# Keeping the first batch on chip in a fused FFT filter and MoE kernel: block transposes on VectorE in place of two trips through DRAM

## The chip, the cores and the metric

The kernel runs on one core of one Trainium2 chip. The metric is the device time of one execution in microseconds (us). Every time below is a median of fast runs; the span that a profile shows is about 2 us shorter than the time of the same run. Kernels that are compared ran on the same chip, with the kernel before run beside them.

A core has a matrix engine (TensorE, "PE" in the profile; its weight loads are "PEld"), VectorE ("DVE"), ScalarE ("ACT"), GpSimd ("POOL") and a queue engine (SyncE, "SP"). A "q" behind a name means the engine's instruction queue, which waits and issues DMAs.

## The reference

```python
# x (8, 3008, 256); filt_r, filt_i (1505, 256); w_in (256, 2048); w_out (2048, 256); alpha (2048,)
X = np.fft.rfft(x, axis=1)
y = np.fft.irfft(X * (filt_r + 1j * filt_i)[None], n=3008, axis=1)   # a circular filter along the sequence
h = y.reshape(24064, 256) @ w_in
s = np.sin(alpha * h)
out = (h + s * s / (alpha + 1e-09)) @ w_out
```

The kernel splits the FFT of length 3008 into 47 x 64. Per batch it does a first small transform (matmul `pa`), a second one with twiddles (`pb`), a product with the filter (`p`), and the two inverses (`pc`, `pd`), whose result `y` feeds the dense part. Between the first and the second transform, and again between the two inverses, the data must change its layout: what was a row index becomes a partition. The kernel before writes to DRAM and reads back for that. The dense part is one hidden matmul (`ph`), a cosine on ScalarE, a "snake" on VectorE (`v`), and a projection (`po`). It works in chunks of 512 tokens, and a chunk is 8 steps. To evict, below, is to copy a matmul's result (`ps`) to a tile that later work reads. The spectral work of a later batch is dealt out between the steps of the dense part of an earlier one, so that TensorE always has something to do. Only batch 0 has nothing to hide behind.

## The kernel before

The order in which batch 0 and batch 1 are worked, with cuts:

```python
FUSED = 2                                   # batches from this one on use the "fused" product
class Spectral:
    def first(self, i):                     # pa, then t1 to DRAM
        ...
        if j == 3:
            nc.sync.dma_start(out=self.d1_rows[:, 8 * ch:8 * ch + 8, :], in_=self.t1)
    def load_t2(self, g): ...               # t2 <- d1, the other layout
    def forward(self, u):                   # pb, evicted to xf
        ...
        if self.fused:                      # the other half of the partitions, by DMA
            for p in range(2):
                nc.sync.dma_start(out=self.xs[u][64 * p:64 * p + 64, :, :],
                                  in_=self.xf[u][64 - 64 * p:128 - 64 * p, :, :])
    def product(self, u):                   # one product if fused, two if not
        for k in range(1 if self.fused else 2): ...
    def cross(self, u):                     # fused: xs * f1, then added to p
        ...
    def inverse(self, w):                   # pc: one matmul a slice if fused, two if not; then g to DRAM
        ...
    def load_t4(self, ch): ...              # t4 <- d2
    def last(self, u): ...                  # pd, evicted to y

def load_x(b, ch):                          # on GpSimd's queue
    ...
    if b == 1: after(ins, marks["t4"])      # a wait
    if b > 2:  after(ins, marks["snake"])   # a wait; batch 2 has none
```

An unfused batch multiplies twice and runs 48 inverse matmuls. A fused batch swaps its two halves of 64 partitions by DMA, does three VectorE operations for each block, and runs 24 inverse matmuls. Before the change batches 0 and 1 are unfused.

## Time and profile before

815.3 us, median of 3 runs (814.78 to 815.31). First, two lines of the page of the kernel before: busy time by engine, and the chain of waits that ended last by engine.

```profile
PE 771.4 (95%) x5649; PEld 527.5 (65%) x5649; DVE 652.4 (80%) x1191; ACT 612.8 (75%) x1200; POOL 65.4 (8%) x111
...
PE 88%; DMA 5%; DVE 2%; ACT 2%; issue 1%; POOL 0%; SPq 0%; ACTq 0%; DVEq 0%; POOLq 0%
```

TensorE is the limit. The table of windows of the kernel before shows where it isn't. A row is a stretch in us, its length, then the busy us of each engine (with the number of instructions), TensorE's granted clock as a share of full speed, the mean busy share of the 16 DMA engines, and the rate.

```profile
core 0: us, PE busy (x) PEld busy (x) DVE busy (x) ACT busy (x) POOL busy (x), PEclk, DMA share, GB/s
...
40.00:60.00 20.00, 10.46 (x65) 5.41 (x64) 12.79 (x25) 8.48 (x18) 3.26 (x5) 0.74 0.88 264
60.00:80.00 20.00, 15.70 (x99) 8.91 (x97) 18.51 (x41) 14.71 (x30) 0.00 (x0) 1.00 0.61 145
80.00:100.00 20.00, 20.00 (x153) 13.91 (x151) 15.79 (x27) 15.41 (x31) 7.39 (x12) 1.00 0.71 174
100.00:120.00 20.00, 20.00 (x151) 14.58 (x150) 17.57 (x36) 16.45 (x33) 0.00 (x0) 1.00 0.58 128
```

From 80 us on TensorE is busy all the time; before that it is not. The timeline of TensorE in the kernel before shows the end of the idle start. Columns: start us, duration us, engine, line, operation, out<-in, shape, count; in brackets the idle time before it and what ended it.

```profile
51.38 0.81 PE L230 MATMUL pd<-wi_t,t 96*128 96x94 f16 x8 [8.56 <-DMA t<-d]
...
53.46 1.01 PE L368 MATMUL ph<-y,w 128*128 128x512 f16 x2 [0.17 <-ACT y L136]
```

TensorE stands still for 8.56 us while batch 0 goes through DRAM the second time, and the first hidden matmul (`ph`) starts at 53.46 us. That start is the number to move: everything after about 80 us is a TensorE that never rests, so a start that is earlier by some us should end the run earlier by as much.

### The profile page before, as it was taken

The page shows a single profiled execution, that of the slowest core. Times are in us where ns is not written, and L with a number is a line of the kernel's source. Part 1 is how long each engine was busy: PE and PEld are TensorE (multiplying, and loading weights), DVE is VectorE, ACT ScalarE, POOL GpSimd, SP SyncE. Part 2 cuts the span into 40 slices and gives each one's busy share as a digit, 9 for nine tenths or more (in the row PEclk, how much of TensorE's full clock was granted, in tenths as well). Part 3 has the DMA queues.
Part 4 walks back from the last instruction along what each step waited for, and adds up shares of the span by engine and source line. Part 5 has one row for each costly group of instructions (what it writes and reads, how often), then busy time and mean ns, then how long its engine had stood idle before and what let it go on. Part 6 is the DMA issues. An engine that isn't in the chain of part 4 may idle for free.

```text
span 812.3 us, 16130 instructions
## 1 busy us (share of the span) xinstructions
PE 771.4 (95%) x5649; PEld 527.5 (65%) x5649; DVE 652.4 (80%) x1191; ACT 612.8 (75%) x1200; POOL 65.4 (8%) x111
## 2 busy tenths in 40 slices
PE   5657999999999999999999999999999999999995
PEld 2324676676666776667667676667667676666674
DVE  3669797789978998789987998779987999777772
ACT  4547787788878888778887887778887887777662
POOL 3210300110020000200002000200002000000000
PEclk9779999999999999999999999999999999999998
DMA  9985755466576465644657554654558333411111
GB/s 213 227 260 132 186 113 148 127 137 141 117 185 149 97 144 126 184 95 95 140 159 178 111 104 116 193 127 104 115 139 214 73 91 84 116 37 40 40 40 46
DMA packets 86201, 104.44 MB, mean 129 GB/s; under 512 B 10388, under 2 KB 72868, under 8 KB 86120
## 3 DMA queue, kind: packets, MB, share of 16 engines
q1 hardware_dynamic: 73904, 73.45, 34.3%
q0 software_dynamic: 10288, 29.11, 18.0%
q10 hardware_dynamic: 1928, 0.86, 0.4%
q8 instruction: 44, 0.72, 0.4%
q14 instruction: 37, 0.30, 0.1%
HBM read 58.02 MB, written 49.81 MB: 133 GB/s over the span
## 4 chain that ended last, share of the span: by engine, by line
PE 88%; DMA 5%; DVE 2%; ACT 2%; issue 1%; POOL 0%; SPq 0%; ACTq 0%; DVEq 0%; POOLq 0%
PE po L383 39%; PE ph L368 38%; PE pa L159 4%; PE pc L210 3%; PE pb L179 3%; PE pd L230 2%; DMA t<-d 2%; DMA x<-in_x_dram 2%; DVE v L372 1%; ACT cos L371 1%; DMA d<-t 1%; ACT t L136 1%; DVE p L193 1%; DMA d<-g 0%; DVE t L138 0%
## 5 line engine op out<-in xcount | busy, mean ns | idle before, releaser
L372 DVE SCALAR_TENSOR_TENSOR v<-cos,ph 128x512 f16<-128x512 f32 (+1 forms) x768 | 483.5, 672 | 119.3 <-ACT cos L371 116.2
L371 ACT ACTIVATE cos<-ph 128x512 f32<-128x512 f32 (+1 forms) x768 | 411.5, 591 | 99.7 <-PE ph L368 98.9
L368 PE MATMUL ph<-y,w 128*128 128x512 f16 (+1 forms) x1536 | 388.5, 375 | 0.8 <-DVE y L138 0.6
L383 PE MATMUL po<-w,v 128*128 128x256 f16 x3008 | 389.0, 272 | 0.0
L383 PEld LDWEIGHTS <-v 128*128 128x128 f16 x3008 | 289.2, 98 | 77.7 <-issue 1.7
L368 PEld LDWEIGHTS <-w 128*128 128x128 f16 x1536 | 148.1, 98 | 104.3 <-issue 3.6
L182 ACT CAST xf<-pb 128x512 f16<-128x512 f32 x96 | 56.9, 594 | 20.4 <-PE pb L179 17.3
L389 ACT COPY o<-po 128x512 f32<-128x512 f32 x96 | 55.6, 579 | 17.9 <-PE po L383 16.3
L136 ACT CAST t<-pa 96x512 f16<-96x512 f32 x88 | 51.2, 585 | 22.8 <-PE pa L159 22.6
L159 PE MATMUL pa<-x,wf_t 94*96 94x512 f16 x128 | 51.0, 408 | 11.7 <-DMA x<-in_x_dram 8.3
L230 PEld LDWEIGHTS <-t 96*128 96x128 f16 x512 | 36.1, 99 | 34.3 <-DMA t<-d 11.0
L170 POOL DMA_DIRECT2D t<-d x56 | 37.0, 676 | 251.1 <-PE ph L368 183.6
L230 PE MATMUL pd<-wi_t,t 96*128 96x94 f16 x512 | 43.0, 208 | 11.5 <-DMA t<-d 10.1
L193 DVE TENSOR_TENSOR p<-xf,filt 128x512 f16<-128x512 f16 x120 | 47.8, 418 | 6.3 <-ACT xf L182 6.1
L136 ACT CAST y<-pd 128x376 f16<-128x376 f32 x82 | 39.3, 480 | 17.0 <-PE pd L230 16.6
L136 ACT CAST g<-pc 128x512 f16<-128x512 f32 x65 | 38.4, 590 | 11.8 <-PE pc L210 11.6
L210 PE MATMUL pc<-p,e_t 128*128 128x256 f16 x240 | 44.0, 278 | 2.7 <-DVE p L193 1.5
L179 PE MATMUL pb<-t,d_t 128*128 128x256 f16 x192 | 38.2, 282 | 5.9 <-DMA t<-d 4.9
L118 POOL DMA_DIRECT2D x<-in_x_dram x32 | 17.0, 536 | 262.8 <-PE pc L210 145.9
L138 DVE CAST t<-pa 96x512 f16<-96x512 f32 x40 | 27.2, 680 | 12.6 <-PE pa L159 12.6
L210 PEld LDWEIGHTS <-e_t 128*128 128x128 f16 x240 | 23.0, 99 | 16.2 <-issue 2.5
L200 DVE TENSOR_TENSOR p<-p,xs 128x512 f16<-128x512 f16 x72 | 30.6, 425 | 2.5
(31 smaller groups left out, 155.2 us busy)
## 6 DMA issues: line engine op xcount, KB each, us to landing
d<-t SPq DMA_DIRECT2D x32, 384.0 KB
d<-g SPq DMA_DIRECT2D x64, 192.0 KB
t<-d SPq DMA_DIRECT2D x32, 384.0 KB
x<-in_x_dram POOLq DMA_DIRECT2D x32, 376.0 KB, 6.2
t<-d POOLq DMA_DIRECT2D x56, 192.0 KB, 7.0
xs<-xf SPq DMA_DIRECT2D x144, 64.0 KB
out_dram<-o SPq DMA_DIRECT2D x72, 94.0 KB
w_in<-in_moe_w_in_dram POOLq DMA_DIRECT2D x2, 1024.0 KB, 8.9
```

Of the source, the lines that this page charges most:

```text
L136: marks["act"] = nc.scalar.copy(out=dst, in_=src)
L159: marks["pe"] = nc.tensor.matmul(out=ps[0:NK, :], lhsT=wf_t, rhs=self.x[ch][:, 2 * j:2 * j + 2, :], start=True, stop=True)
L179: nc.tensor.matmul(out=ps[:, i, :], lhsT=d_t[:, s, :], rhs=self.t2[s // 6][:, s % 6, :], start=True, stop=True)
L182: nc.scalar.copy(out=self.xf[u], in_=ps)
L193: marks["prod", u] = nc.vector.tensor_tensor(out=pt, in0=self.xf[u], in1=f_t[k][:, 2 * u:2 * u + 2, :], op=ALU.mult)
L210: nc.tensor.matmul(out=ps[:, i, :], lhsT=e_t[:, k, 2 * w + i, :], rhs=pt[:, i, :], start=(k == 0), stop=(k == len(pr) - 1))
L230: nc.tensor.matmul(out=psv[:, i, :], lhsT=self.t4[ch][:, 4 * half + i, cb * 128:cb * 128 + 128], rhs=wi_t, start=True, stop=True)
L368: nc.tensor.matmul(out=ps[:, 0:n], lhsT=w1[:, cb, jb * 128:jb * 128 + 128], rhs=y_cols[:, cb, c0:c0 + n], start=(cb == 0), stop=(cb == 1))
L371: nc.scalar.activation(out=cs[:, 0:n], in_=ps[:, 0:n], func=AFT.Sin, bias=float(np.pi / 2))
L372: marks["snake"] = nc.vector.scalar_tensor_tensor(out=v[k][:, jb, 0:n], in0=cs[:, 0:n], scalar=-1.0, in1=ps[:, 0:n], op0=ALU.add, op1=ALU. ...
L383: nc.tensor.matmul(out=pso[k][:, t % 2, :], lhsT=v[k][:, jb, 128 * t:128 * t + 128], rhs=w2[:, jb, :], start=(jb == 0), stop=(jb == 15))
L389: nc.scalar.copy(out=o[:, 0:nb, :], in_=pso[k][:, 0:nb, :])
```

## The change

The intent: batch 0 does not leave the chip. Its two changes of layout are done by VectorE as transposes of 32x32 blocks of 32-bit words, each word a pair of fp16 channels. Buffers are shared so that all of it fits; for lack of room the second inverse table of batch 0 lies in a buffer that is needed later, so batch 1 can't use it and becomes fused. Some VectorE work of the start moves to GpSimd: one of the filter copies, the six multiplies that scale `w_in` by alpha, half of the scaling of `w_out`. All engines now run in the order of emission. The core of the diff, with cuts:

```diff
-FUSED = 2
+FUSED = 1
...
+    def turn(dst, src, c0):
+        nc.vector.transpose(out=dst[:, :, c0 % 128:c0 % 128 + 64].bitcast(UINT32).rearrange("p s c -> p c s"),
+                            in_=src.bitcast(UINT32).rearrange("p s c -> p c s"))
...
+    for c0 in (0, 64, 128, 192):
+        turn(t2_0[c0 // 128], t1_0[:, :, c0:c0 + 64], c0)
+    blocks = [(hc, w) for w0 in (0, 3) for hc in range(2) for w in range(w0, w0 + 3)]
...
+    def weights_in(g):
+        js, w32 = w_in32[g]
+        eng = nc.vector if g in () else nc.gpsimd
+        eng.tensor_tensor(out=w1[:, :, js], in0=w32, in1=cos_cols[:, None, js]..., op=ALU.mult)
...
+    for i in range(-1, 12 + 3):                       # batch 0: forward, product, inverse, block by block
+        ... other_half(...)                           # filter copies: i = -1 two on VectorE; i = 5 one on GpSimd, one on VectorE
+        forward_0(i); product_0(i - 1); inverse_0(i - 3)      # in bounds
+        if i == 6:
+            for g in (0,1,2,6,7,8,9,3,4,5):           # w1 multiplies; 6 to 9 are batch 1's x loads
+                ...
+        if i - 3 == 8 + 2:
+            turn_back(0)
+            turn_back(64)
+    turn_back(128)
+    turn_back(192)
...
-                put(13.6 if b == 2 else zp + -44 + 7 * ch, s.load_x, ch)
+                put(2 + 8 + 0.6 if b == 2 else zp + -44 + 7 * ch, s.load_x, ch)
...
-            inv = 22.5 + u if b == 1 else 59 + 2.1 * u if b == 2 else z + -40.8 + 2.3 * u
-            fwd = inv - (1.5 if b == 1 else 6)
+            inv = 17 + 5 + u if b == 1 else 59 + 2.1 * u if b == 2 else z + -40.8 + 2.3 * u
+            fwd = inv - (5 if b == 1 else 6)
...
+                put(fwd + (3 if b == 1 else 4.5), s.cross, u)
```

## The prediction

> **What bounds the kernel now.** TensorE, after a slow start. The window table shows PE busy 97-100% of every stretch from 80 us to 780 us, at full granted clock; before 70 us it is busy about 50 us. Counting columns at 2.4 per ns, the work is about 743 us (estimate from the group list's shapes and counts); about 39 us of it is done by 80 us. So 41 us are lost in the first 80 us, about 17 us in the long middle, 11 us at the end. In the timeline the first hidden matmul (ph) starts at 53.5 us and the first projection at 69.2 us. Before that the chain of waits runs x DMA, first transform (to 17.0), d<-t 4.9 us and t<-d 4.3 us through DRAM, products and inverse (27.0 to 42.8), then d<-g 3.2 us and t<-d 3.8 us: PE stands still 8.6 us before the first pd. Batch 1's x loads cost another 2.1 us at 63.9.
>
> **Removed.** Batch 0's DRAM round trips (about 5.5 and 8.6 us of dead time on the chain, 6.3 MB of DMA traffic while the DMA share is 0.8 to 1.1), the DVE half of the e table; DVE loses the eight w1 multiplies (4.9 us) and half of the w2 scaling (about 2.7 us) to GpSimd; batch 1 loses 24 inverse matmuls (2.6 us of PE), but the second e table by PE adds about as many columns, early, and three ACT evictions (1.02 us).
>
> **Added.** Eight VectorE block transposes of 1024 32-bit elements. The Trainium skill, Vector Engine (DVE) Microarchitecture Reference, section 3.8, says the transpose sustains one element per cycle per lane; no trace here shows it yet. The trace's f32 128x512 multiply takes 0.61 us back to back, so I estimate 1.2 us per transpose, 10 us in all; the last two stand on the chain. GpSimd multiplies: GPSIMD Engine Reference, section 3, has tensor_tensor at about half of VectorE's speed, so about 1.5 to 2 us per w1 group, 10 us, finishing near 40 us, just before the fourth cosine slot, which holds alpha, is needed. Batch 1 gains two VectorE ops per block (24 x 0.42 us, minus 12 products) and 24 swap DMAs.
>
> **Timeline after (estimate).** x landed 11.9; first transform evicted near 16; d_t about 18.5; transposes to 21; then ACT is the limit: 24 evictions of 0.59 plus three tables, 17 us, to 40; two transposes, last, evictions: ph starts at about 44.5, 9 us earlier. Chunk 0 stays VectorE/ACT-bound (15.7 us before, about 15 after). Later stretches are PE-saturated, so the gain stays, with one repayment: batch 1 still does one block per step, where VectorE needs about 2.5 us per step against 2.15 us of PE, so the saved inverse matmuls are not cashed in and 1 to 3 us are lost.
>
> **Predicted: 805.5 us, 8 in 10 between 798 and 811.5; faster by over 2%: 0.14, within 2%: 0.83, slower: 0.03.**
>
> **Shown by:** first ph near 44.5 us; transposes near 1.2 us each; no d<-t, d<-g before it; DMA share lower before 45 us; PE over 95% from about 70 us; VectorE near 100% in batch 1's blocks with PE idle on products or cosines.
>
> **What would make it wrong:** strided 32-bit access making transposes two or more times slower (ph near 49, 809 us); GpSimd slower, holding the cosine slots (later); ACT and VectorE overlapping better, or batch 1 swaps fitting without stall (799 or below).

## More of the kernel before

One more view, the groups of VectorE instructions between 25 and 56 us, for the cost of the filter products and copies before. After the count come the busy us and the mean ns of one.

```profile
L193 DVE TENSOR_TENSOR p<-xf,filt 128x512 f16<-128x512 f16 x24 | 8.7, 420 | 6.3 <-ACT xf L182 6.1
...
L274 DVE COPY filt<-filt 64x1536 f16<-64x1536 f16 x3 | 1.7, 576 | 0.1
```

Back to back they overlap a little: 24 products occupy 8.7 us, 0.36 us each.

## The result, and the profile after

The changed kernel takes 827.79 us (median of 4 runs, 826.39 to 829.48) against 815.3. The ratio is 1.0155, with a 95% interval from 1.0135 to 1.0176: slower by 1.5%, clear of noise, and outside of the predicted range. A ratio here and below is the mean time of one kernel's fast runs over that of the other's of the same rounds, so not quite the ratio of the medians.

The page of the changed kernel, the same two lines:

```profile
PE 778.1 (94%) x5745; PEld 533.0 (65%) x5745; DVE 673.5 (82%) x1187; ACT 617.3 (75%) x1206; POOL 79.1 (10%) x115
...
PE 80%; DVE 7%; DMA 6%; ACT 2%; issue 2%; SPq 1%; POOL 0%; ACTq 0%; DVEq 0%; POOLq 0%
```

VectorE has come onto the chain (2% before, 7% now). To see when the time is lost, compare the two traces at the same place in the program. The dense part is the same 4544 matmuls in the same order in both kernels, so the start of the k-th of them can be set against each other. This table is worked out from the traces; "e15" is the last experiment's kernel, discussed at the end.

| k-th dense matmul | before, us | after, us | difference | e15, us | difference |
|---|---|---|---|---|---|
| 0 (first `ph`) | 53.5 | 55.8 | +2.4 | 47.1 | -6.4 |
| 180 | 94.9 | 96.8 | +1.9 | 87.1 | -7.8 |
| 220 | 101.6 | 111.5 | +9.9 | 93.8 | -7.9 |
| 340 | 125.3 | 136.8 | +11.5 | 119.5 | -5.9 |
| 600 | 169.6 | 180.6 | +10.9 | 164.7 | -4.9 |
| 4543 (last) | 803.7 | 816.7 | +13.0 | 799.7 | -4.1 |

Two things went wrong, and both are early. The dense part starts 2.4 us later instead of 9 us earlier. And 8.0 us are lost between the matmuls 180 and 220, around 100 us. After that the two kernels run alike: the difference grows by another 3.1 us over 700 us.

**The start.** TensorE's timeline of the changed kernel, at the lines that answer to those shown of before:

```profile
51.08 0.81 PE L246 MATMUL pd<-wi_t,t_h 128*128 128x94 f16 x8 [3.53 <-DVE t_h L329]
55.18 0.88 PE L246 MATMUL pd<-wi_t,t_h 128*128 128x94 f16 x8 [3.29 <-DVE t_h L329]
...
55.85 0.63 PE L455 MATMUL ph<-y,w 128*128 128x512 f16 x1
```

The wait for DRAM is gone. A wait for the transposes stands in its place. The groups of VectorE between 17 and 56 us show what VectorE did until then:

```profile
L368 DVE TENSOR_TENSOR p<-xf,filt 128x512 f16<-128x512 f16 x24 | 15.0, 682 | 0.7 <-issue 0.4 <-ACT xf L361 0.2
L329 DVE STREAM_TRANSPOSE t_h<-t_h 128x1024 uint32<-128x1024 uint32 x4 | 8.3, 2180 | 0.0
L329 DVE STREAM_TRANSPOSE t<-t 128x1024 uint32<-128x1024 uint32 x2 | 4.3, 2222 | 0.0
L329 DVE STREAM_TRANSPOSE t_h<-t 128x1024 uint32<-128x1024 uint32 x2 | 3.7, 1925 | 0.4 <-ACT t L148 0.4
L325 DVE TENSOR_SCALAR filt<-filt 64x3072 f16<-64x3072 f16 x2 | 3.5, 1742 | 0.1
```

VectorE is busy without a break and is the limit of the start. A transpose takes 1.9 to 2.2 us, where the prediction had 1.2, and the same 24 products occupy 15.0 us, where they had 8.7 before.

**The stall.** The windows of the changed kernel:

```profile
40.00:60.00 20.00, 12.13 (x115) 8.74 (x114) 16.87 (x24) 10.28 (x21) 3.59 (x5) 0.68 0.04 8
60.00:80.00 20.00, 16.98 (x101) 8.98 (x100) 17.44 (x34) 17.05 (x36) 0.00 (x0) 1.00 0.20 60
80.00:100.00 20.00, 20.00 (x155) 14.10 (x154) 14.79 (x25) 14.25 (x29) 7.40 (x12) 1.00 0.86 192
100.00:120.00 20.00, 13.88 (x93) 9.04 (x92) 13.40 (x29) 12.37 (x25) 0.00 (x0) 0.83 0.34 88
```

From 100 to 120 us TensorE is busy for 13.88 us of 20, where it had been busy all the time. Look at the column of the DMA share too. Before, it was 0.88 in the stretch from 40 to 60 us; now the DMA engines do next to nothing there (0.04), and they are fuller than before from 80 to 100 us (0.86 against 0.71). The traffic was not only taken away, it was pushed together. The timeline and the waits of the changed kernel around 100 us (in the waits: who waited for whom, us in total, times, longest):

```profile
88.61 9.99 SPq L488 DMA_DIRECT2D out_dram<-o  x5
98.70 6.11 SPq L196 DMA_DIRECT2D xs<-xf  x6
...
DVE xs L209 <- DMA xs<-xf: 9.3, 2, 7.9
ACT xf L192 <- DMA xs<-xf: 8.9, 2, 8.4
PE pd L246 <- ACT xf L192: 6.0, 1, 6.0
```

`xs<-xf` is the half swap of batch 1, new with the change. SyncE's queue issues it at 98.70 us, behind output stores, the last of which took 8.58 us to issue; its second half lands at 106.15 us by the chain of waits. Until then ScalarE may not overwrite `xf`, and TensorE waits for ScalarE. In the same time batch 1's `t2` loads land (88 to 94.5 us) and the four loads of batch 2's `x` (96.3 to 102.8 us).

### The profile page after: what moved, and what is told of

Same layout as the page of the kernel before. It is cut to its first block, busy times and chain, and to the rows that moved or that the text cites. A ratio compares the mean times of both kernels' runs of the same rounds, so it can differ in the third digit from the quotient of the medians.

```text
span 825.4 us, 16345 instructions
## 1 busy us (share of the span) xinstructions
PE 778.1 (94%) x5745; PEld 533.0 (65%) x5745; DVE 673.5 (82%) x1187; ACT 617.3 (75%) x1206; POOL 79.1 (10%) x115
## 4 chain that ended last, share of the span: by engine, by line
PE 80%; DVE 7%; DMA 6%; ACT 2%; issue 2%; SPq 1%; POOL 0%; ACTq 0%; DVEq 0%; POOLq 0%
PE po L470 36%; PE ph L455 34%; DMA t_h<-d 3%; PE pd L246 3%; PE pa L169 2%; PE pc L220 2%; DVE v L459 2%; PE pb L189 2%; DMA filt<-in_filt_i_dram 2%; SPq L488 1%; DVE t_h L329 1%; ACT cos_all L458 1%; DMA xs<-xf 1%; DVE p L368 1%; PE pc L378 1%
## 5 line engine op out<-in xcount | busy, mean ns | idle before, releaser
L459 DVE SCALAR_TENSOR_TENSOR v<-cos_all,ph 128x512 f16<-128x512 f32 (+1 forms) x768 | 483.2, 671 | 116.4 <-ACT cos_all L458 113.1
L458 ACT ACTIVATE cos_all<-ph 128x512 f32<-128x512 f32 (+1 forms) x768 | 411.6, 591 | 103.0 <-PE ph L455 102.0
L246 PEld LDWEIGHTS <-t_h 96*128 96x128 f16 (+1 forms) x512 | 35.6, 99 | 39.8 <-issue 7.8
L246 PE MATMUL pd<-wi_t,t_h 96*128 96x94 f16 (+1 forms) x512 | 43.0, 208 | 16.5 <-DVE t_h L329 6.8
L148 ACT CAST t_h<-pa 96x512 f16<-96x512 f32 x75 | 43.9, 587 | 10.2 <-PE pa L169 9.9
L169 PE MATMUL pa<-x,wf_t 94*96 94x512 f16 x112 | 42.3, 381 | 2.7 <-ACT t_h L148 2.5
L209 DVE TENSOR_TENSOR xs<-xs,filt 128x512 f16<-128x512 f16 x84 | 35.0, 417 | 9.3 <-DMA xs<-xf 9.3
L220 PE MATMUL pc<-p,e_t 128*128 128x256 f16 x168 | 32.4, 275 | 3.5 <-DVE p L210 3.4
L203 DVE TENSOR_TENSOR p<-xf,filt 128x512 f16<-128x512 f16 x84 | 35.0, 416 | 0.1
L220 PEld LDWEIGHTS <-e_t 128*128 128x128 f16 x168 | 15.6, 98 | 15.7 <-DVE p L210 4.2
```

What stands on the lines that cost most here:

```text
L148: marks["act"] = nc.scalar.copy(out=dst, in_=src)
L169: marks["pe"] = nc.tensor.matmul(out=ps[0:NK, :], lhsT=wf_t, rhs=self.x[ch][:, 2 * j:2 * j + 2, :], start=True, stop=True)
L220: nc.tensor.matmul(out=ps[:, i, :], lhsT=e_t[:, 2 * w + i, :], rhs=pt[:, i, :], start=(k == 0), stop=(k == len(pr) - 1))
L246: nc.tensor.matmul(out=psv[:, i, :], lhsT=lhsT, rhs=wi_t if self.b else wi0_t, start=True, stop=True)
L458: nc.scalar.activation(out=cs[:, 0:n], in_=ps[:, 0:n], func=AFT.Sin, bias=float(np.pi / 2))
L459: marks["snake"] = nc.vector.scalar_tensor_tensor(out=v[k][:, jb, 0:n], in0=cs[:, 0:n], scalar=-1.0, in1=ps[:, 0:n], op0=ALU.add, op1=ALU. ...
```

## The experiments

The theories for the start: the w1 multiplies on GpSimd slow VectorE (theory C), against products that are slow of themselves (D); and for the transposes strided access (E) against a slow operation (F). For the stall: the swaps wait behind loads on full DMA engines (A), against the fused form as such, its VectorE load or its short distance (B). Times of the kernel before beside each group of runs were 814.8 to 815.2 us. A run where nothing else is said gave the right result.

### e1_x2_late: batch 2's loads put later in the program

```diff
-                put(2 + 8 + 0.6 if b == 2 else zp + -44 + 7 * ch, s.load_x, ch)
+                put(24 if b == 2 else zp + -44 + 7 * ch, s.load_x, ch)
```

> One edit: batch 2's x loads are issued at step 24 instead of 10.6. Theory A (the 6.05 us TensorE stall at 100.5 us comes from batch 1's half swaps, whose DMAs wait behind batch 2's x loads and batch 1's loads on full DMA engines): the stall shrinks to under 2 us and the time falls 5 to 8 us, to about 820. Rival B (the stall is the fused form itself: too few steps between forward and cross, or VectorE load): the stall stays near 6 us and the time stays 826 to 829.

829.77 us, ratio 1.0177 (1.0154 to 1.0199). It decides nothing, because the edit did not do what it was meant to. The trace shows the loads issued at 91.3 to 94.1 us, still right behind the `t2` loads: GpSimd's queue has nothing else to wait for and runs ahead, so the place in the program sets only the order within this queue. To move such a load it must be made to wait for something.

### e2_no_swap: batch 1 without its swap

```diff
-            if self.fused:
+            if b == 1:
+                self.xs[u] = xspool.tile(...)            # no DMA
+            elif self.fused:
...
-        nc.vector.tensor_tensor(out=xs, in0=xs, in1=f_t[1]..., op=ALU.mult)
+        nc.vector.tensor_tensor(out=xs, in0=self.xf[u] if self.b == 1 else xs, in1=f_t[1]..., op=ALU.mult)
```

> Batch 1 leaves its half swap out and multiplies the unswapped tile (wrong result on purpose; VectorE work unchanged, 24 DMAs gone). Theory A: no stall at 100 us, time about 818 to 819. Rival B (VectorE load of the fused form): stall or its equivalent of several us stays between 95 and 135 us, time 825 or more.

Its output is wrong, which doesn't matter for the time. 821.91 us, 1.0078 (1.0055 to 1.0100). The stall is gone: the difference to the kernel before is +4.3 us at matmul 180 and +5.1 at 220. So the swap's DMA is what the stall waits for, and VectorE's load is not, because its work is unchanged. The load has a smaller price: the difference rises to +8.0 us by matmul 280 and falls back to +6.4 by 400, and the time is 3 us above what theory A gave. The short distance between `forward` and `cross` this run doesn't decide; e6 below keeps the distance, and its stop at 100 us is gone.

### e3_w1_on_vector and e4_no_w1_multiply: GpSimd's multiplies

```diff
-        eng = nc.vector if g in () else nc.gpsimd
+        eng = nc.vector
```

> The six w1 multiplies go from GpSimd to VectorE (about 5 us more VectorE work before the first hidden matmul). Theory C (GpSimd's two-input multiplies slow VectorE's two-input products and filter copies in 23 to 37 us): products take 0.36 to 0.45 us each instead of 1.08, the first ph starts about 3 us earlier than 55.9, time about 825. Rival D (the products are slow for another reason): products stay near 1 us, first ph starts about 5 us later, time about 832.

```diff
-        ins = nc.sync.dma_start(out=w_in32[g][1], in_=w_in_v[:, :, js])
+        ins = nc.gpsimd.dma_start(out=w1[:, :, js], in_=w_in_v[:, :, js])      # casts; alpha is left out
...
-        eng.tensor_tensor(out=w1[:, :, js], in0=w32, in1=..., op=ALU.mult)
+        return
```

> w_in is cast straight into w1 by DMA, nobody multiplies by alpha (wrong result on purpose). Theory C: products near 0.4 us, first ph near 48 us, time about 820. Rival D (what counts is the transposes, four of them on the chain at the end): first ph stays within 2 us of 55.9.

e3: 825.54 us, 1.0124 (1.0106 to 1.0143), first `ph` at 53.5 us. e4 (wrong): 818.27 us, 1.0037 (1.0015 to 1.0059), first `ph` at 48.2 us. The group of products between 17 and 56 us in e3:

```profile
L368 DVE TENSOR_TENSOR p<-xf,filt 128x512 f16<-128x512 f16 x24 | 9.1, 434 | 2.2 <-ACT xf L361 2.1
```

With no w1 multiplies on GpSimd beside them the products are back at their length (9.1 us for 24, 15.0 in the changed kernel), and so are the filter copies (0.95 us; 1.97 and 2.44 in the changed kernel). Theory C holds, D falls. The Trainium skill, GPSIMD Engine Reference, section 1 (Specifications), says that GpSimd's SBUF interface is shared with VectorE, with contention when a VectorE instruction has two SBUF inputs or runs in a two-port mode; the trace agrees and puts a size on it. In the changed kernel the first eight products took 8.65 us beside the multiplies, against 2.96 us of work in e3. There is a scatter on top: in runs with an unchanged start these eight took between 8.4 and 11.5 us, and the first `ph` came at 55.5 us with the short ones (e9) and 58.2 us with the long ones (e12). The single instructions of the traces show where it comes from, and that the w1 multiplies are not alone: behind them GpSimd scales half of `w_out`. In e12 it did seven of these eight in 0.47 us each while one product took 4.12 us; in the changed kernel they took 0.7 to 1.2 us each, and the products beside them 0.4 to 0.7 us. One engine waits for the other, and which of them it is changes from run to run.

The transposes, on the other hand, were not slowed: the second pair took 4.3 us beside GpSimd's filter copy and first multiplies (the changed kernel) and without the multiplies (e3, e4).

### e5_transpose_cost: five operations measured by themselves

```diff
+    nc.vector.transpose(out=flat(dst_f), in_=flat(src_f))        # L357: flat: 1024 words in a row
+    nc.vector.transpose(out=flat(dst_f), in_=tall(src_t))        # L358: tall: as in turn()
+    nc.vector.transpose(out=tall(dst_t), in_=flat(src_f))        # L359
+    nc.vector.transpose(out=..., in_=...)                        # L360: the same bytes as 2048 fp16, flat
+    nc.vector.tensor_copy(out=tall(dst_t), in_=tall(src_t))      # L362
     for c0 in (0, 64, 128, 192):
```

> Before the first four transposes stand five extra VectorE operations on the same data, whose results are overwritten (result stays right): transposes of 1024 32-bit elements with (1) flat source and flat destination, (2) strided source, flat destination, (3) flat source, strided destination, (4) 2048 16-bit elements, both flat, and (5) a plain copy of 1024 32-bit elements with both patterns strided. Theory E (the strides of 256 and 512 bytes cost): (1) about 1.2 us, (2) or (3) and (5) near 1.9 to 2.1 us. Rival F (the transpose itself takes about two cycles per 32-bit element): (1), (2), (3) all 1.85 to 2.2 us, (5) 0.6 to 1.2 us.

Only a look (one run, state unknown; durations in the trace are what counts). The groups of VectorE between 17 and 27 us:

```profile
L360 DVE STREAM_TRANSPOSE t_h<-t 128x2048 f16<-128x2048 f16 x1 | 2.3, 2311 | 0.0
L329 DVE STREAM_TRANSPOSE t_h<-t 128x1024 uint32<-128x1024 uint32 x1 | 2.0, 1951 | 0.0
L358 DVE STREAM_TRANSPOSE t_h<-t 128x1024 uint32<-128x1024 uint32 x1 | 1.9, 1922 | 0.1
L359 DVE STREAM_TRANSPOSE t_h<-t 128x1024 uint32<-128x1024 uint32 x1 | 1.9, 1917 | 0.0
L357 DVE STREAM_TRANSPOSE t_h<-t 128x1024 uint32<-128x1024 uint32 x1 | 1.2, 1235 | 0.0
L362 DVE COPY t_h<-t 128x1024 uint32<-128x1024 uint32 x1 | 1.0, 1023 | 0.0
```

A flat transpose takes 1.235 us, as predicted. One strided side makes it 1.92 us, and the second adds nothing (1.95). F falls, because (1) is short, and E holds for the transposes; pairs of channels are the right unit: the same bytes as fp16 take 2.31 us. But E missed the plain copy: with both patterns strided it took only 1.02 us, as F had it, where E expected 1.9 to 2.1. So it is the transpose for which these strides are shown to cost. The Trainium skill, SBUF — State Buffer, in its note on cachelines, says that each access that crosses to a new 16-byte line pays a penalty. That fits the transposes with strides of 256 and 512 bytes here in direction; whether the copy pays too is not shown, because no flat copy was measured.

e5 also speaks for C, unasked: its extra work put the products behind GpSimd's w1 multiplies (over at 36.3 us; the products start at 37.16), and the first eight took 2.95 us of work.

### e11_flat_transposes: all eight transposes flat

```diff
-        nc.vector.transpose(out=dst[:, :, c0 % 128:c0 % 128 + 64].bitcast(UINT32).rearrange("p s c -> p c s"), ...)
+        nc.vector.transpose(out=dst[:, r0:r0 + 16, :].bitcast(UINT32).rearrange("p s (a b) -> p (s a) b", b=32), ...)
```

> The changed kernel with all eight transposes on flat patterns, of other data (wrong result on purpose). Theory E (strides): each takes about 1.24 us instead of 1.9 to 2.2; the last four save 3.7 us directly, the first four may be eaten up by GpSimd's multiplies, so the first ph moves 4 to 7 us earlier and the time is 821 to 824. If ph moves less than 2 us, the transposes were not on the chain.

Its output is wrong, which doesn't matter for the time. 823.39 us, 1.0099 (1.0077 to 1.0120), first `ph` at 50.9 us: 4.9 us earlier. The eight transposes take 9.3 us in all (16.3 in the changed kernel). But the eight products behind the first four now took 11.35 us: they start earlier and meet more of GpSimd's multiplies. What the first four save is eaten up there, and what the last four save (3.7 us) counts.

### e6_x2_gated, e9_x2_after_swaps, e12_x2_after_last_swap: moving the loads for real

All three give batch 2's loads something to wait for. In e6 they wait for the snakes of steps 24 to 30 one by one, in e9 all for the snake of step 29, in e12 for the last swap of batch 1:

```diff
-        if b > 2:
+        if b > 1:
             after(ins, marks["snake"])                    # e12: marks["swap"] for batch 2
...
+                put(24 + 2 * ch if b == 2 else ...)       # e6;  e9: 29.5;  e12: 28.6
```

> Batch 2's x loads carry a wait on the snake of steps 24, 26, 28 and 30, as later batches' loads do (moving the issue alone did not move them, because the GpSimd queue runs ahead). Theory A: the swaps of batch 1 land within 2 to 3 us of their issue, the 6 us stall falls under 1.5 us, time 6 to 8 us below the changed kernel's, about 820. Rival B (latency of the swap itself): stall over 4 us stays, time over 825.

> Batch 2's x loads are gated behind step 29.5, after the last swap of batch 1 (in e6 they fell among the later swaps and the stall moved from 100 to 128 us). Theory A: neither stall appears; the time falls 7 to 9 us below the changed kernel's, to 819 to 821. If a stall of 4 us or more remains between 95 and 140 us, the loads are not its cause.

> The changed kernel; batch 2's x loads wait for the last swap of batch 1 to land. In e9 the gate was one step too early: two of the swaps (issued at about the same time as the loads) still landed late, and a stall of 6.2 us came at 125 us. Theory A: no stall over 2 us between 95 and 135 us; time 818 to 821. Rival: a stall stays or comes elsewhere (batch 2's first transform waits for x); time 824 or more.

| kernel | x loads issued, us | longest stops of TensorE | time, us (ratio, 95% interval) |
|---|---|---|---|
| after | 88.6 to 91.3 | 6.05 us at 101 | 827.79 (1.0155, 1.0135 to 1.0176) |
| e6 | 112.9 to 127.9 | 4.07 us at 128 | 824.78 (1.0123, 1.0091 to 1.0155) |
| e9 | 121.8 to 123.7 | 5.99 us at 125 | 826.41 (1.0143, 1.0128 to 1.0158) |
| e12 | 129.4 to 131.2 | 1.93 us at 133 and 4.29 us at 145 | 831.85 (1.0204, 1.0186 to 1.0221) |

TensorE's timelines at those stops, of e9 and then of e12:

```profile
131.14 0.58 PE L220 MATMUL pc<-p,e_t 128*128 128x256 f16 x2 [5.99 <-DVE p L210]
```

```profile
135.02 0.42 PE L169 MATMUL pa<-x,wf_t 94*96 94x512 f16 x1 [1.93 <-DMA x<-in_x_dram]
...
148.81 0.34 PE L246 MATMUL pd<-wi_t,t_h 96*128 96x94 f16 x4 [4.29 <-DMA t_h<-d]
```

Each time the stall at 100 us is gone, and each time it comes back where the loads now are: first among the later swaps (VectorE waits for `xs<-xf`, TensorE for VectorE), then, behind all swaps, in batch 2's own first transform and in batch 1's second trip through DRAM (`t_h<-d`). So theory A is right about the mechanism, and its repair is not one: in none of the three places did four loads, which took 4.8 to 11.5 us each to land (e6 and the changed kernel), go in among batch 1's DMAs (loads of `t2`, 24 swaps, `g` out, `t4` in) without a stop. Other places were not tried. All expectations that the time would fall to 818 to 821 missed. By the rule for e9, its stop of 5.99 us would clear the loads. I don't read it so, because e9's loads were issued in the middle of its last swaps (121.2 to 125.2 us), and e12, whose loads wait for the last swap, has no wait for a swap of over 1.4 us between 95 and 135 us.

### e7_swap_on_act_queue: the swaps on another queue

```diff
-                    nc.sync.dma_start(out=self.xs[u]...)
+                    (nc.scalar if b == 1 else nc.sync).dma_start(out=self.xs[u]...)
```

> Batch 1's swaps are issued from ScalarE's queue instead of SyncE's, behind no output store; x loads of batch 2 stay where they are. Theory A1 (the swap is late because it stands in SyncE's queue behind an output store whose issue is held 8.6 us): swap issued within 1 us of its xf, stall under 2 us, time about 820. Theory A2 (all 16 DMA engines are full of loads; the queue does not matter): the swap lands at about the same time, stall of 4 us or more stays, and ScalarE itself may be held by the issue; time 825 to 830.

841.98 us, 1.0355 (1.0320 to 1.0391), the worst kernel. ScalarE's timeline in e7:

```profile
97.56 0.59 ACT L192 CAST xf<-pb 128x512 f16<-128x512 f32 x1
104.72 1.12 ACTq L196 DMA_DIRECT2D xs<-xf  x2
105.93 0.58 ACT L476 COPY o<-po 128x512 f32<-128x512 f32 x1 [7.78 <-issue]
```

No output store stands before the swaps now, and still the third pair is issued 6.6 us after its `xf`; meanwhile ScalarE does nothing for 7.78 us. The queue was not the cause, A2 holds (though its 825 to 830 us was far too low), and an engine that computes was made to stand in line. The Trainium skill, Trainium Kernel Development and Optimization, Key Constraints, says that the queues all run on the same 16 DMA engines and that issuing from several engines only saves issue time; this run fits: the first multiply with a swapped half started at 108.2 us, 106.2 in the changed kernel. What exactly holds the issue, the trace does not show.

### e8_gated_and_w1_vector and e10_repaired: repairs together

e8 is e6 with e3's edit. e10 is e9 with w1 groups 0 to 2 on VectorE and 3 to 5 on GpSimd behind the last product, the halves of the channels one after the other, and the first two back-transposes earlier.

> Both repairs together: batch 2's x loads gated and the w1 multiplies on VectorE. If the two causes are separate and add: about 827.8 - 7 - 2.3 = 818; if one hides the other: no better than the better one alone, 820 or more.

> e9 plus three repairs of batch 0: w1 groups 0 to 2 on VectorE and 3 to 5 on GpSimd only after the last product; the channel halves one after the other instead of alternating; the first two back-transposes between the products. Expected from e4 and e9: first ph near 48 us, no stall, 810 to 813 us, below the kernel before. If ph starts early and the time still is not below 815, the late losses of batch 1's fused form decide.

e8: 820.46 us, 1.0070 (1.0055 to 1.0085), better than either edit alone, so neither cause hides the other; it stays above the 818 of the sum, and its trace still loses 8.2 us between the matmuls 280 and 340, where e6's loads now are. e10: 822.38 us, 1.0085 (1.0066 to 1.0105), first `ph` at 52.6 us, not 48, and a stop of 6.38 us at 123 us, as in e9. Both misses.

### e13_front_repaired and e14_b1_unfused

Both have all four filter copies on GpSimd and all w1 multiplies on GpSimd behind the last product; e13 has e12's loads, e14 an unfused batch 1. For the second inverse table e14 keeps a tile of its own, which fits because two pools lose a buffer each:

```diff
-FUSED = 1
+FUSED = 2
+    e1_t = cpool.tile([128, NS, 128], FP16)                    # the second inverse table, kept
-    gpool = pool("gp", 4);  opool = pool("op", 3)
+    gpool = pool("gp", 3);  opool = pool("op", 2)
-            inv = 17 + 5 + u if b == 1 ...;  fwd = inv - (5 if b == 1 else 6)
+            inv = 22.5 + u if b == 1 ...;    fwd = inv - (1.5 if b == 1 else 6)
```

> e12 plus batch 0 repaired further: all four filter-half copies on GpSimd before the products, all w1 multiplies on GpSimd after the last product (during the last transposes), channel halves one after the other. First ph at 48 to 50 us; with no stall the time is 811 to 815.

> e13's batch 0, but batch 1 with two products and 48 inverse matmuls as in the kernel before, no swaps, second table kept in its own tile (g pool 3 instead of 4 buffers, o pool 2 instead of 3), batch 2's x loads where the change has them. First ph as in e13; nothing lost between 95 and 140 us against the kernel before; 809 to 812, unless the smaller pools stall.

e13: 831.01 us, 1.0190 (1.0170 to 1.0209). e14: 820.04 us, 1.0059 (1.0046 to 1.0073). The first `ph` came at 54.8 and 54.9 us, not at 48 to 50: the repair had a fault of its own. GpSimd's timeline in e13:

```profile
13.67 2.74 POOL L323 COPY filt<-filt 64x3072 f16<-64x3072 f16 x1 [0.95 <-DMA filt<-in_filt_r_dram]
18.05 7.97 POOL L325 TENSOR_SCALAR filt<-filt 64x3072 f16<-64x3072 f16 x1 [1.64 <-DMA filt<-in_filt_i_dram]
26.08 3.00 POOL L323 COPY filt<-filt 64x3072 f16<-64x3072 f16 x1
29.16 8.01 POOL L325 TENSOR_SCALAR filt<-filt 64x3072 f16<-64x3072 f16 x1
```

and VectorE's beside it:

```profile
25.60 10.79 DVE L368 TENSOR_TENSOR p<-xf,filt 128x512 f16<-128x512 f16 x6
```

The copy with a change of sign takes GpSimd 7.97 us, where the plain copy takes 2.74 and VectorE 0.95. The products start on time, but of the six in this line one took 2.96 us beside the second copy and one 6.43 us beside the second change of sign. It is the contention of theory C again, now from the filter copies. Both times missed. But e14 answers its question: at matmuls 0, 180 and 220 it is +1.4, +0.9 and +0.9 us behind the kernel before. An unfused batch 1 has no stall, with batch 2's loads where the change has them.

### e15_gated_w1_unfused, e16_alpha_later, e17_only_front_repaired

e15 is the changed kernel with e14's batch 1 and this:

```diff
-            for g in (0,1,2,6,7,8,9,3,4,5):          # at i == 6
+            for g in (6, 7, 8, 9):                   # batch 1's x loads alone
...
+    for g in range(6):                               # behind the loop, still on GpSimd
+        weights_in(g)                                # the first one waits for the last product of batch 0
     turn_back(128)
     turn_back(192)
     s0.last(0, True)
-    s0.last(2, False)
+    s0.last(2, True)                                 # one eviction goes to ScalarE (in e10, e13 and e14 too)
```

e16 moves the alpha broadcasts behind the first transform as well. e17 is e16 with the change's fused batch 1.

> The changed kernel with (a) all six w1 multiplies still on GpSimd but waiting for batch 0's last product, so that they run beside the last transposes, filter copies as in the change; (b) batch 1 unfused as in e14. From e4 (first ph 48.2 us without w1 multiplies) and e14 (about 2 us lost by 140 us): first ph 48 to 49, products near 0.4 us, no stall over 1 us before 140 us, time 812 to 814, below the kernel before. If one of the causes is not the cause, the time stays at 816 or more.

> e15 with the alpha broadcasts (5.8 us of TensorE before the first transform at 10.0 us, while x lands from 6.0 us) moved behind the first transform: transposes start near 14.5 instead of 17.7 us, first ph near 46 us, time 810 to 812.

> e16's front with the change's fused batch 1 and its early x loads: the stall near 90 us is back, time 6 to 8 us above e16. If it is within 2 us of e16, the stall was not worth its length.

e15: 812.64 us (810.71 to 813.12) against 814.8 of the kernel before in the same rounds, ratio 0.9965 (0.9953 to 0.9977). Faster than both kernels, if by little. The group of products between 17 and 56 us, and the start of the dense part on TensorE's timeline, in e15:

```profile
L369 DVE TENSOR_TENSOR p<-xf,filt 128x512 f16<-128x512 f16 x24 | 8.7, 421 | 0.6 <-ACT xf L362 0.4
...
47.11 0.63 PE L459 MATMUL ph<-y,w 128*128 128x512 f16 x1
```

The products take 8.7 us again. GpSimd's six multiplies ran from 38.16 us for 9.65 us, beside the last transposes, which took 8.5 us, hardly more than in e3 (8.3). So this is where the multiplies belong: next to VectorE instructions that they don't slow. The first `ph` starts 6.4 us earlier than before, and there is no stop over 1.1 us up to 140 us (the longest is 1.08 us; the kernel before has one of 2.11).

e16: 812.76 us, 0.9971 (0.9956 to 0.9986). The first `ph` came at 46.1 us, but the microsecond was lost again by matmul 400; it gains nothing over e15 and misses its 810 to 812 by a little. e17: 823.17 us, 1.0091 (1.0078 to 1.0105), 10.4 us more than e16 in the same rounds, with TensorE waiting 8.0 us in one piece around 93 us. That is the price of fusing batch 1 here, with the start repaired, and more than the 6 to 8 us expected. In the two profiles the stall is the larger part: between the matmuls 180 and 220 e17 loses 11.0 us against the kernel before, and e16 nothing. But e17's first `ph` came at 49.5 us, 3.3 us later than e16's, and why is not shown.

## Why the prediction was wrong

- **"ph starts at about 44.5 us, 9 us earlier": wrong, 55.85 us.** The removed waits for DRAM were real. Three terms of the sum on VectorE were mis-sized. "I estimate 1.2 us per transpose, 10 us in all" holds only for flat patterns: 1.235 us there, 1.9 to 2.2 us with the strides of this kernel, 16.3 us in all. The products were costed at their old length: 24 of them took 15.0 us instead of 8.7, because of GpSimd's arithmetic beside them (e3, e4, e15). The filter copies beside them took 1.97 and 2.44 us instead of 0.95. And all four back-transposes stood on the chain, 8.3 us, where I had put two, 2.4 us. By stages: the first transposes ended at 25.7 us (21 predicted), the products at 46.9 (40), and the first `ph` started at 55.85 (44.5).
- **GpSimd "finishing near 40 us, just before the fourth cosine slot ... is needed": right and beside the point.** It finished the w1 multiplies at 36.6 us. I asked only when GpSimd would be done, not whom it would slow down while it worked.
- **"then ACT is the limit" of the products: wrong.** VectorE was busy without a break; in e15, with the contention gone, it still is nearly so.
- **"Later stretches are PE-saturated, so the gain stays": right.** From matmul 400 to 800 the difference to the kernel before moves by 0.3 us, and e15's gain of 4.8 us there is nearly the whole gain at the end (4.1). In the changed kernel another 1.9 us go from matmul 800 to the end.
- **"the saved inverse matmuls are not cashed in and 1 to 3 us are lost", by VectorE's load: the size was wrong and the cause only a small part.** 8.0 us went in one piece, between the matmuls 180 and 220. The cause is the swaps' DMAs among other loads, which e2, e6, e9, e12 and e17 show. I had named the 24 swap DMAs as added and gave them no time. VectorE's load costs little: in e2, without swap DMAs, 2.1 us more by matmul 400 than at 180.
- **"DMA share lower before 45 us": wrong.** It was 0.98 and 1.05 in the first two stretches of 20 us, and fell to 0.04 only in the third.
- Of the reasons that I gave in advance for being wrong, the first (strided transposes) was among the causes. The second was not: GpSimd was in time for the cosine slots, and that it would slow VectorE is nowhere in the prediction. And the one that cost most was on the other side of the list: I had counted swaps that fit "without stall" as good luck, and not swaps that don't fit as bad luck.
- That the time would stay within 2% was given 0.83 and came true, but as a loss of 1.5% where a gain of 1.2% was expected. That is luck.

Left open: what holds a DMA's issue while the loads are under way (8.58 us for a store on SyncE's queue, 6.6 us on ScalarE's), and why a transpose with two strided sides costs no more than one with one.

## What to carry to other kernels

When DMA traffic is removed in one place, look at where the remaining traffic goes: here it was pushed together into the stretch where a later batch needed short, urgent DMAs, and moving the bulk loads to three other places only moved the stall. Work that is moved to GpSimd to relieve VectorE may cost VectorE more than it saves; put it beside VectorE instructions that it does not slow, and measure those by their length in the trace. Price an operation with the access pattern that it will have, not with its number of elements.

## What the Trainium skill lacked or had wrong

- Vector Engine (DVE) Microarchitecture Reference, section 3.8: one element per cycle per lane for a transpose agrees with 1.235 us for 1024 flat 32-bit elements, twice the 0.61 us of the f32 multiply of 512. It has no price of strides for a transpose (the page's section 5.2 has measured prices of single-element hops, for an elementwise operation): 1.92 us with one strided side, 1.95 us with both, up to 2.2 us in the other transposes of these kernels; and 2.31 us for the same bytes as 2048 flat fp16 elements.
- GPSIMD Engine Reference, section 1: the contention with VectorE is named without a size (how the two block each other stands in SBUF — State Buffer, Who interferes with whom). Eight fp16 products of 128x512 took 8.65 us and up to 11.5 us beside GpSimd's arithmetic, and 2.84 us in e15 without it. Transposes were not slowed (4.3 us a pair in both cases).
- GPSIMD Engine Reference, section 4.1, calls one-input operations roughly line-rate. That doesn't hold for every one of them: a copy of 64x3072 fp16 took 2.74 us (0.89 ns an element of a row), the same with a multiply by -1 took 7.97 us (2.59 ns).
- Trainium Kernel Development and Optimization, Key Constraints, is right about shared DMA engines, and lacks that the issue of a small DMA can hold its queue for microseconds, as it did here while loads were under way: 8.58 us on SyncE's queue, 6.6 us from the eviction to the issue on ScalarE's, with ScalarE idle for 7.78 us.
- No page was found to say that a load's place in the program does not delay it when its queue has nothing else to wait for (e1: issued at 91.3 us, right behind the loads before it, although it was placed 13 steps later).
